# Gated rows summed on TensorE, both diagonal spectrum products on VectorE, and a planner that follows the buffers' turns

## The chip, the core and the metric

The kernel runs on one core of a Trainium2 chip. A core has TensorE (PE in the profile, with its weight loads as PEld), VectorE (DVE), ScalarE (ACT), GpSimd (POOL), and SyncE (SP), which issues most of the DMAs. The metric is the device time of one launch in microseconds. Before the change the median of three runs is 759.34 us (757.93 to 760.80).

## The reference

Four layers act on a sequence of 2048 positions and 512 channels. Layers A (gated) and B (a state-space filter made from exponentials) alternate; both end in a causal convolution over the whole sequence, done by a Fourier transform of length 4096.

```python
def _A_ref(q, k, v, shift_k, ssm_k, ssm_D):
    k_pad = jnp.pad(k, ((0, 0), (ks - 1, 0), (0, 0)))
    k_shift = jnp.zeros_like(k)
    for t in range(ks):                                   # ks = 4
        k_shift = k_shift + k_pad[:, t:t + S, :] * shift_k[:, ks - 1 - t][None, None, :]
    kv = k_shift * v
    ...                                                   # y = long convolution of kv with ssm_k
    y = y + kv * ssm_D[None, None, :]
    return q * y

def _B_ref(u, log_A_real, A_imag, C_real, C_imag, log_dt, D_skip):
    ...                                                   # C = (C_real + i C_imag) dt
    P = jnp.exp((A * dt[:, None])[:, :, None] * pos[None, None, :])
    K = 2.0 * jnp.einsum("dn,dnl->dl", C, P).real
    ...                                                   # y = long convolution of u with K
    return y + u * D_skip[None, None, :]

x = A_q
x = x + _A_ref(_layernorm(x, axis=-1), A_k, A_v, A_shift_k, A_ssm_k, A_ssm_D)
x = x + _B_ref(_layernorm(x, axis=-1), ...)
x = x + _A_ref(_layernorm(x, axis=-1), A_k, A_v, A_shift_k, A_ssm_k, A_ssm_D)
x = x + _B_ref(_layernorm(x, axis=-1), ...)
```

In layer A the sequence that is convolved, `kv`, depends on the inputs alone, not on x. So the long convolution of A is computed once and used by both A layers. The "gated rows" of this document are `kv`: four shifted copies of k, each times a tap, summed, and the sum times v.

## The kernel before

The program has three parts.

1. A short opening in program order: it loads the filter parameters and prepares rates and phases (line 177 in the profile, where operations are issued as they are recorded).
2. A planned part. Here every operation is only recorded (`Planner.record`), and `flush` issues them all in an order that `plan` works out (line 319 in the profile). Two generators feed it, interleaved by `run_steps`. The first, `stream`, builds the filter taps of layer B in 64 units, and then their spectra. The second, `diagonal`, makes the gated rows and the spectra of A's filter, and then runs A's long convolution.
3. The two B layers with the second A update between them, again in program order (line 177).

One unit of `taps` goes through these tiles: `pa` (angles, PSUM, two buffers) from a matmul, rounded by VectorE to `y`, `y` subtracted by a second matmul with `minus`, a negative unit matrix; ScalarE turns `pa` into sines and cosines (`ab`, `tt`); VectorE makes `e2` and GpSimd the two halves of `xy`; a contraction on TensorE sums them in `pk`. Eight units are a round; before each round six exponentials `m` are made from matmuls `pm`. A spectrum is made of `kk` (input), `pf` and `pu` (matmul results), `zk` (transposed) and `pc` (stored to `spec`).

The gated rows come in 16 groups of 32 channels. `gated` loads a tile `kvt` of 39 rows (19 of k, 16 of v, 4 of taps) and does eight elementwise operations of 128 by 512 elements on it: four products with the taps, three sums and the product with v. The mask `KVE` puts operations 1, 2, 4 and 7 on GpSimd and the others on VectorE, for 15 groups; the first group is all on GpSimd. Each operation reads what the one before it wrote in `u` or `tb`.

The long convolution (`convolution`, with `inplace` for A) takes pairs of frequency chunks: a matmul result `pu`, the diagonal products with the filter spectrum `kab`, a second matmul `pi`, a copy back, a transpose `w`, and the result `po`. The spectrum has two parts: ScalarE copies `pu` to the tile `sw` and GpSimd multiplies `sw` by one part, while VectorE multiplies `pu` by the other part into `vv`.

The planner takes a cost for each operation (`cost`) and goes through time: for each engine it takes the recorded operation that can start first, and the earliest of these is placed next. A tile can start when its tag has a free buffer; before the change it counts free buffers of a tag, in whatever order they come free. PSUM has one bank of tag `c1` (here for `po`), two double banks of tag `f1`, two of `pa` and one of `pk`.

Of the kernel before, what the change touches and what calls it, by code (L numbers as in the profile page):

```python
# [108 lines left out]
class Planner:  # L109
# [69 lines left out]

    def cost(self, op):  # L180
        name, a, k = op.calls[0]
        aps = [x for x in list(a) + list(k.values()) if hasattr(x, "tensor")]
        free = lambda x: int(np.prod([c for _, c in x.ap[1:]])) if len(x.ap) > 1 else 1
        n = max(free(x) for x in aps)
        if name == "dma_start":
            size = 4 * int(np.prod([c for _, c in aps[0].ap]))
            return (450 if op.engine == "D" else 600), 1500 + size / 290, size
        big = [x for x in aps[1:] if free(x) > 1]
        psum = [x.space == PSUM for x in big]
        if op.engine == "T":  # L190
            total, each = 0, 0
            for _, b, _ in op.calls:
                d = free(b[2]) * (1 if b[2].dtype == F32R else 4) / 2.4
                area = b[1].ap[0][1] * free(b[1]) / 16384
                total, each = total + d * area, max(each, d)
            return max(total, each), max(total, each) + 230, 0
        if op.engine == "V":
            alone = len(big) == 1 and not psum[0] and name in ("tensor_copy", "tensor_scalar", "tensor_scalar_mul")
            o = 60 + n * (0.52 if alone else 1.06)
            return o, o + 85, len(big) > 1 and not any(psum)  # L200
        if op.engine == "S":
            o = n / 1.2 + (50 if all(psum) else 184)
            if any(hasattr(k.get(x), "tensor") for x in ("scale", "bias")):
                o = n / 1.2 + (186 if name == "activation" and len(big) == 1 else 280)
            return o, o + 105, 0
        o = 100 + 2.2 * n if name.startswith("tensor_tensor") or name in ("tensor_mul", "tensor_add", "tensor_sub") else 100 + 0.9 * n
        return o, o + 50, n > 1

    def plan(self):
        ops = self.ops  # L210
        last_use, slots, queue = {}, {}, {}
        for op in ops:
            for t in op.uses:
                last_use[t.name] = op.n
        pending = [len(op.before) + len(op.ordered) for op in ops]
        follow = [[] for _ in ops]
        for op in ops:
            for o in list(op.before) + op.ordered:
                follow[o.n].append(op)
        users = {}  # L220
        for op in ops:
            for t in op.uses:
                users.setdefault(t.name, []).append(op.n)
                if len(users[t.name]) == 1 and t.tag_meta is not None:
                    queue.setdefault(t.tag, []).append(t)
        left = {n: len(u) for n, u in users.items()}
        taken = {tag: 0 for tag in queue}
        head = {tag: 0 for tag in queue}
        owner = {n: u[0] for n, u in users.items()}
        live = set()  # L230
        free = {e: 0.0 for e in self.engines}
        ready = [0.0] * len(ops)
        start, end = {}, {}
        avail = {e: [] for e in self.engines}
        lanes, server, lock = [0.0] * 8, 0.0, {"V": 0.0, "G": 0.0}
        costs = [self.cost(op) for op in ops]
        frees = {tag: [] for tag in queue}
# [3 lines left out]
        waiting = len(ops)  # L241
        while waiting:
            best = None
            for e, l in avail.items():
                pick = None
                for n in l:
                    op, t = ops[n], max(free[e], ready[n])
                    ok = True
                    for u in op.uses:
                        if u.name in live or u.tag_meta is None:  # L250
                            continue
                        tag = u.tag
                        q = queue[tag]
                        if q[head[tag]].name != u.name:
# [6 lines left out]
                        fr = frees[tag]  # L261
                        if len(fr) and u.tag_meta.bufs - taken[tag] <= len(fr):
                            t = max(t, sorted(fr)[0])
                    if not ok:
                        continue
                    if e == "D":
                        t = max(t, min(lanes))
                    if costs[n][2] and e in "VG":
                        t = max(t, lock["G" if e == "V" else "V"])
                    if pick is None or (t, n) < pick:  # L270
                        pick = (t, n)
                if pick is not None and (best is None or pick[0] < best[0]):
                    best = (pick[0], pick[1], e)
            assert best is not None, "plan is stuck"
            t, n, e = best
            op = ops[n]
            avail[e].remove(n)
            for u in op.uses:
                if u.name not in live and u.tag_meta is not None:
                    live.add(u.name)  # L280
                    taken[u.tag] += 1
                    head[u.tag] += 1
                    fr = frees[u.tag]
                    if len(fr) and u.tag_meta.bufs - taken[u.tag] < len(fr):
                        fr.remove(min(fr))
            o, lat, extra = costs[n]
            start[n] = t
            free[e] = t + o
            end[n] = t + lat
            if e == "D" or op.calls[0][0] == "dma_start":  # L290
                server = max(server, t + o) + extra / 290
                end[n] = max(t + o + 1500, server + 1200)
                if e == "D":
                    i = lanes.index(min(lanes))
                    lanes[i] = end[n]
            elif extra and e in "VG":
                lock[e] = t + o
            for u in op.uses:
                left[u.name] -= 1
                if not left[u.name] and u.tag_meta is not None:  # L300
                    taken[u.tag] -= 1
                    frees[u.tag].append(end[n])
            for f in follow[n]:
                pending[f.n] -= 1
                ready[f.n] = max(ready[f.n], end[n] + self.RELEASE[f.engine] if op in f.before else start[n] + o)
                if not pending[f.n]:
                    avail[f.engine].append(f.n)
            waiting -= 1
        self.length = max(end.values())
        return sorted(range(len(ops)), key=lambda n: (start[n], n))  # L310

    def flush(self):
        last = {}
        for n in self.plan():
# [16 lines left out]
def kernel(ctx: ExitStack, tc: tile.TileContext, out, x_in, kv_in, ssmk_in, ssmd_in,  # L331
# [174 lines left out]
    def convolution(which, pools, steps, finish, lag, ahead, nk, ns, nw, inplace, zlast=None, late_step=None, first_b=False):  # L506
# [12 lines left out]
        for s in range(-2 * NCH, NS + lag + NCH + 1):  # L519
# [312 lines left out]
    with ExitStack() as actx:  # L832
# [31 lines left out]
        KVE = 0b10010110  # L864
# [6 lines left out]
        def kv_steps():  # L871
            for grp in range(KV0, 16):
                yield from gated(grp, KVE)
# [54 lines left out]
        def diagonal():  # L928
            kvs = kv_steps()
            for q in range(NQ):  # L930
                for i, _ in enumerate(spectrum_quarter(0, q, ssmk_in, ap, zlast, ZA)):
                    if q == 0 and i == 1:
                        for grp in range(KV0):
                            for _ in gated(grp, 255):
# [271 lines left out]
```

## Time and profile before

| | |
|---|---|
| median of three runs | 759.34 us |
| the profiled execution | 758.29 us, of which its span 756.2 us |
| mean granted TensorE clock | 0.814 |
| opening, until the first exponentials | 0 to 48.7 us |
| rounds 1 to 4 of the taps, with the gated rows | 48.7 to 262 us |
| rounds 5 to 8, with A's long convolution from about 300 us on | 262 to 510 us |
| both B layers, second A update | 510 to 756 us |

The profile's page gives busy times and shares of the span. A row of the view by stretches has the stretch, its length, the busy time of PE, PEld, DVE, ACT and POOL with the count of instructions in brackets, the granted TensorE clock as a share of full speed, the DMA share and the bytes moved. A row of the groups has engine, operation, tiles, shapes and count, then the busy time of all, the mean ns of one, and the idle time of that engine just before them with what ended it. A row of the waits has who waited for whom, the us in total, how often, and the longest.

### The profile page before, as it was taken

Reading aid. Unit: us, or ns where it says so; the run is one execution under the profiler, and the core shown is the slowest. Engines: PE = TensorE matmul, PEld = TensorE weight load, DVE = VectorE, ACT = ScalarE, POOL = GpSimd, SP = SyncE. Lnnn points to the kernel's source line nnn. Section 1 sums busy time; section 2 is a strip of 40 time slices with the busy share of each in tenths; the row PEclk is TensorE's granted clock in tenths of the full one; section 3 lists DMA queues with packets and bytes.
Section 4 is the critical chain, followed back from the end, with each engine's and each line's share of the span. In section 5 each row is a group of like instructions: output and inputs, shape, how many; then the busy total and the mean of one; then the engine's idle time right before and its main releaser. Section 6 shows DMA issues by size and latency. Waiting matters only on the chain. (4 is left out here: it accounts for less than half of the span.)

```text
span 756.2 us, 20631 instructions
## 1 busy us (share of the span) xinstructions
PE 527.1 (70%) x8440; PEld 306.3 (40%) x8440; DVE 513.7 (68%) x930; ACT 421.1 (56%) x784; POOL 407.6 (54%) x378
## 2 busy tenths in 40 slices
PE   1356476467778688698877878563798880689984
PEld 0024243223426344464343455331465640256662
DVE  6765876748764458366777728764578889978864
ACT  4138447437547777975746388234673436837441
POOL 3756868688676576575448248500454530255551
PEclk9998565566665559889997879865999996889999
DMA  9888986346556315366577566669587713057764
GB/s 250 232 201 215 295 195 210 99 114 177 154 164 203 130 49 147 89 226 212 148 212 227 184 158 193 178 213 280 213 295 227 254 60 135 0 198 251 260 204 98
DMA packets 74497, 138.93 MB, mean 184 GB/s; under 512 B 8092, under 2 KB 37156, under 8 KB 72356
## 3 DMA queue, kind: packets, MB, share of 16 engines
q1 hardware_dynamic: 73540, 135.21, 60.0%
q0 software_dynamic: 864, 2.43, 1.1%
q8 instruction: 66, 1.08, 0.6%
q14 instruction: 27, 0.22, 0.1%
HBM read 97.75 MB, written 39.85 MB: 182 GB/s over the span
## 5 line engine op out<-in xcount | busy, mean ns | idle before, releaser
L319 POOL TENSOR_TENSOR xy<-tt,m 128x512 f32<-128x512 f32 x128 | 152.9, 1217 | 74.0 <-issue 30.1
L177 POOL TENSOR_TENSOR sw<-sw,kab 128x512 f32<-128x512 f32 x64 | 80.7, 1281 | 118.2 <-ACT sw L177 117.1
L319 ACT ACTIVATE m<-pm 128x1024 f32<-128x1024 f32 x48 | 46.7, 1029 | 66.3 <-PE pm L319 66.2
L319 PE MATMUL pf<-kk,w 64*128 64x512 f32 x128 | 57.3, 945 | 34.3 <-POOL kk L319 18.5
L319 PE MATMUL pk<-xy,e 128*32 128x64 f32 x2048 | 56.4, 271 | 20.2 <-POOL xy L319 18.5
L319 DVE TENSOR_TENSOR e<-pa,m 128x512 f32<-128x512 f32 x64 | 43.7, 682 | 38.8 <-ACT pa L319 15.9
L319 PE MATMUL pa<-tt,rw 64*128 64x512 f32 x64 | 41.4, 650 | 35.1 <-DVE e L319 34.1
L177 ACT COPY ie<-pi 128x1024 f32<-128x1024 f32 x32 | 32.5, 1014 | 57.4 <-PE pi L177 57.4
L319 PEld LDWEIGHTS pk<-xy,e 128*32 128x32 f32 x2048 | 43.3, 140 | 51.0 <-POOL xy L319 26.7
L177 DVE TENSOR_TENSOR vv<-pu,kab 128x512 f32<-128x512 f32 x64 | 40.9, 677 | 31.1 <-ACT sw L177 28.4
L319 ACT ACTIVATE ab<-pa 128x512 f32<-128x512 f32 x64 | 38.3, 598 | 39.0 <-PE pa L319 38.9
L319 DVE TENSOR_SCALAR y<-pa 128x512 fp32r<-128x512 f32 x64 | 43.5, 682 | 23.7 <-PE pa L319 22.5
L319 POOL TENSOR_TENSOR sw<-sw,kab 128x512 f32<-128x512 f32 x32 | 40.5, 1284 | 34.5 <-ACT sw L319 28.7
L319 DVE STREAM_TRANSPOSE zk<-pf 128x512 f32<-128x512 f32 x64 | 41.8, 690 | 24.0 <-PE pf L319 24.0
L319 POOL TENSOR_TENSOR u<-u,tb 128x512 f32<-128x512 f32 x32 | 44.3, 1388 | 24.3 <-DVE u L319 11.5
L177 PE MATMUL pf<-u,w 64*128 64x512 f32 (+1 forms) x136 | 39.6, 676 | 24.7 <-ACT u L177 17.0
L319 PE MATMUL pa<-y,minus 128*128 128x512 f32 x64 | 40.3, 629 | 23.1 <-DVE y L319 22.9
L177 PE MATMUL pi<-sw,mm 64*64 64x128 f32 x1024 | 52.3, 269 | 2.9 <-issue 2.9
L177 PE MATMUL pi<-vv,mm 64*64 64x128 f32 x1024 | 52.9, 274 | 0.5 <-DVE vv L177 0.4
L319 PE MATMUL pu<-zk,w 64*64 64x128 f32 x1024 | 48.6, 347 | 3.8 <-ACT m L319 1.5
L177 ACT COPY sw<-pu 128x1024 f32<-128x1024 f32 x32 | 32.3, 1014 | 29.8 <-PE pu L177 29.8
L319 PEld LDWEIGHTS pu<-zk,w 64*64 64x64 f32 x1024 | 40.3, 177 | 17.6 <-issue 10.1
(140 smaller groups left out, 1246.3 us busy)
## 6 DMA issues: line engine op xcount, KB each, us to landing
kab<-spec SPq DMA_DIRECT2D x94, 512.0 KB, 4.8
spec<-pc SPq DMA_DIRECT2D x64, 256.0 KB, 3.0
kvt<-kv_in SPq DMA_DIRECT2D x32, 312.0 KB, 5.2
kk<-ssmk_in SPq DMA_DIRECT2D x32, 128.0 KB, 3.6
xr<-x_in SPq DMA_DIRECT2D x8, 512.0 KB, 5.9
kv_d<-u SPq DMA_DIRECT2D x16, 256.0 KB, 4.2
kdram<-ks SPq DMA_DIRECT2D x64, 64.0 KB, 4.1
kk<-kdram SPq DMA_DIRECT2D x32, 128.0 KB, 3.0
```

The source lines that it names most:

```text
L177: op.ins = getattr(self.engines[key], name)(*a, **k).ins
L319: ins = getattr(self.engines[op.engine], name)(*a, **k).ins
```

## The change

It has three parts.

- `gated`: GpSimd makes the four products with the taps, each into its own half of two tiles (`prod`). TensorE adds them: four matmuls with `minus`, read as plain f32, accumulate the negative sum in a PSUM bank `kv` of tag `c1`. VectorE multiplies that by -1 and by v in one operation, and the result is stored. The mask is gone; all 16 groups go this way.
- `convolution`, for A alone: VectorE makes both diagonal products from `pu` in PSUM. The copy to `sw` by ScalarE and the product by GpSimd are gone there. The B layers are as before.
- `Planner`: a tile now waits for that earlier tile of its tag whose buffer it gets in turn (`prior`). The cost of a matmul depends on an assumed TensorE clock of 0.5 or 1 that follows the matmul work in windows of 3413 ns, and that of a DMA on the length of its runs. So the order of the whole planned part is another.

The third part of the program has the same instructions in the same order as before.

```diff
+    @staticmethod
+    def run(ap):
...
-            return (450 if op.engine == "D" else 600), 1500 + size / 290, size
+            run = min(self.run(x) for x in aps)
+            return (450 if op.engine == "D" else 600), 1500 + size / 290, size / (290 if run >= 512 else 200)
...
-            return max(total, each), max(total, each) + 230, 0
+            return max(total, each), 230, total
...
-    def plan(self):
+    def prepare(self):
...
+                    q = self.queue.setdefault(t.tag, [])
+                    self.prior.append(q[-t.tag_meta.bufs] if len(q) >= t.tag_meta.bufs else None)
+                    q.append(len(self.prior) - 1)
...
+    def plan(self, rank=None):
...
+                    for u in using[n]:
+                        if live[u] or prior[u] is None:
                             continue
...
-                        room = u.tag_meta.bufs - taken[tag]
-                        if room <= 0:
-                            ok = False
-                            break
...
+                        if left[prior[u]]:
                             ok = False
                             break
+                        t = max(t, idle[prior[u]] + self.RELEASE[e])
...
+            if e == "T":
+                k = int(t / 3413)
+                while window < k:
+                    clock = 1.0 if act.get(window, 0.0) >= 0.42 * 3413 else 0.5
+                    window += 1
+                o = o / clock
...
@@ convolution
-                    swapped[0] = S.copy(vvs[s // 2][1], pus[0])
+                    if not inplace:
+                        swapped[0] = S.copy(vvs[s // 2][1], pus[0])
                 wa, wb = vvs[s // 2]
-                G.tensor_mul(wb[:, c % 2], wb[:, c % 2], kabs[s][:, 1])
+                if inplace:
+                    V.tensor_mul(wb[:, c % 2], pus[0][:, c % 2], kabs[s][:, 1])
+                else:
+                    G.tensor_mul(wb[:, c % 2], wb[:, c % 2], kabs[s][:, 1])
                 V.tensor_mul(wa[:, c % 2], pus[0][:, c % 2], kabs[s][:, 0])
...
-        def gated(grp, onpool):
+        def gated(grp):
             kvt = ap.tile([128, 39, 32], F32, name="kvt", tag="kab", bufs=NKA)
             by_half(kvt.rearrange("p t c -> p (t c)"), kv_in[grp])
-            u = ap.tile([128, 16, 32], F32, name="u", tag="vv", bufs=NSA // 2)
-            tb = ap.tile([128, 16, 32], F32, name="tb", tag="sw", bufs=NSA // 2)
-            e = [G if (onpool >> i) & 1 else V for i in range(8)]
-            sk = lambda j: kvt[:, 35 + j, :][:, None, :].to_broadcast([128, 16, 32])
-            kt = lambda j: kvt[:, j:j + 16, :]
-            e[0].tensor_mul(u, kt(3), sk(0))
-            e[1].tensor_mul(tb, kt(0), sk(3))
-            e[2].tensor_add(u, u, tb)
+            prods = [ap.tile([128, 2, 16, 32], F32, name="prod", tag=tag, bufs=NSA // 2) for tag in ("vv", "sw")]
+            kv = bank("kv")
+            for j in range(4):
+                G.tensor_mul(prods[j // 2][:, j % 2], kvt[:, 3 - j:19 - j, :],
+                             kvt[:, 35 + j, :][:, None, :].to_broadcast([128, 16, 32]))
+                T.matmul(kv, minus.bitcast(F32), prods[j // 2][:, j % 2].rearrange("p t c -> p (t c)"),
+                         start=j == 0, stop=j == 3)
+                if j % 2:
+                    yield
+            u = prods[0][:, 0].rearrange("p t c -> p (t c)")
+            V.scalar_tensor_tensor(u, kv, -1.0, kvt[:, 19:35, :].rearrange("p t c -> p (t c)"), op0=ALU.mult, op1=ALU.mult)
+            Q.dma_start(kv_d[grp], u)
             yield
-            e[3].tensor_mul(tb, kt(1), sk(2))
-            e[4].tensor_add(u, u, tb)
-            yield
-            e[5].tensor_mul(kt(2), kt(2), sk(1))
-            e[6].tensor_add(u, u, kt(2))
-            e[7].tensor_mul(u, u, kt(19))
-            Q.dma_start(kv_d[grp], u.rearrange("p t c -> p (t c)"))
-            yield
```

More of the change, by code (lines that the diff above doesn't have):

```diff
@@ L178, in record @@
         return op
+    @staticmethod
+    def run(ap):
+        dims = [tuple(d) for d in ap.ap] if ap.space == DRAM else [tuple(d) for d in ap.ap[1:]]
+        n = 1
+        for s, c in reversed(dims):
+            if c > 1 and s != n:
+                break
+            n *= c
+        return n
     def cost(self, op):
@@ L207, in cost @@
         return o, o + 50, n > 1
-    def plan(self):
+    def prepare(self):
         ops = self.ops
-        last_use, slots, queue = {}, {}, {}
+        self.costs = [self.cost(op) for op in ops]
+        self.follow = [[] for _ in ops]
         for op in ops:
-            for t in op.uses:
[L214 to L231, printed above, removed]
+            for o in op.before:
+                self.follow[o.n].append((op.n, True))
+            for o in op.ordered:
+                self.follow[o.n].append((op.n, False))
+        self.pending = [len(op.before) + len(op.ordered) for op in ops]
+        names, self.prior, self.queue = {}, [], {}
+        self.using, self.users = [], []
+        for op in ops:
+            l = []
+            for t in op.uses:
+                if t.tag_meta is None:
+                    continue
+                if t.name not in names:
+                    names[t.name] = len(self.prior)
+                    q = self.queue.setdefault(t.tag, [])
+                    self.prior.append(q[-t.tag_meta.bufs] if len(q) >= t.tag_meta.bufs else None)
+                    q.append(len(self.prior) - 1)
+                    self.users.append(0)
+                l.append(names[t.name])
+                self.users[names[t.name]] += 1
+            self.using.append(l)
@@ L235, in plan @@
         lanes, server, lock = [0.0] * 8, 0.0, {"V": 0.0, "G": 0.0}
-        costs = [self.cost(op) for op in ops]
-        frees = {tag: [] for tag in queue}
+        act, window, clock = {}, 0, 0.5
         for op in ops:
@@ L240, in plan @@
                 avail[op.engine].append(op.n)
-        waiting = len(ops)
-        while waiting:
+        for waiting in range(len(ops)):
             best = None
@@ L277, in plan @@
             avail[e].remove(n)
[L278 to L285, printed above, removed]
+            for u in using[n]:
+                live[u] = True
             o, lat, extra = costs[n]
@@ L297, in plan @@
                 lock[e] = t + o
[L298 to L307, printed above, removed]
@@ L308, in plan, with best @@
-            waiting -= 1
-        self.length = max(end.values())
+            for u in using[n]:
+                left[u] -= 1
+                idle[u] = max(idle[u], end[n])
+            for f, real in self.follow[n]:
+                pending[f] -= 1
+                ready[f] = max(ready[f], end[n] + self.RELEASE[ops[f].engine] if real else start[n] + o)
+                if not pending[f]:
+                    avail[ops[f].engine].append(f)
+        self.length = max(end)
         return sorted(range(len(ops)), key=lambda n: (start[n], n))
+    def best(self):
+        return self.plan()
@@ L312, in flush @@
     def flush(self):
         last = {}
-        for n in self.plan():
+        self.prepare()
+        for n in self.best():
             op = self.ops[n]
@@ L872, in kv_steps @@
             for grp in range(KV0, 16):
-                yield from gated(grp, KVE)
+                yield from gated(grp)
         def steps_a(q):
```

59 lines of the change are left out of this document (33 added, 26 removed).

## The prediction

> **What bounds the kernel now.** I read the page's shares first, then the busy time in four stretches: opening, taps with gated rows (48.7 to 262), taps with the first long convolution (262 to 510), the rest.
>
> ```profile
> span 756.2 us, 20631 instructions
> PE 527.1 (70%) x8440; PEld 306.3 (40%) x8440; DVE 513.7 (68%) x930; ACT 421.1 (56%) x784; POOL 407.6 (54%) x378
> ```
> ```profile
> core 0: us, PE busy (x) PEld busy (x) DVE busy (x) ACT busy (x) POOL busy (x), PEclk, DMA share, GB/s
> 0.00:48.70 48.70, 11.31 (x20) 3.40 (x21) 30.90 (x45) 11.36 (x17) 25.50 (x37) 1.00 0.87 230
> 48.70:262.00 213.30, 145.49 (x1748) 80.47 (x1745) 140.03 (x207) 127.57 (x264) 155.18 (x133) 0.65 0.64 179
> 262.00:510.00 248.00, 192.81 (x3323) 113.61 (x3323) 160.65 (x292) 159.59 (x299) 136.60 (x130) 0.84 0.58 172
> 510.00:756.20 246.20, 177.47 (x3352) 108.78 (x3352) 182.12 (x389) 122.54 (x205) 90.33 (x79) 0.90 0.59 191
> ```
>
> No engine is full. POOL leads the second stretch (155.2 of 213.3, 73%), PE the third (78%). The change leaves the last stretch as it is, so about 246 us can't move. What stands between POOL and full in the second stretch, by the waits there:
>
> ```profile
> ACT m L319 <- PE pm L319: 64.2, 9, 26.0
> POOL u L319 <- DVE u L319: 33.4, 13, 5.8
> POOL u L319 <- DVE tb L319: 8.9, 4, 3.3
> ```
>
> POOL waits 42.3 us (33.4 + 8.9) for VectorE inside the gated rows. ACT's 64.2 us are its pauses between rounds of eight units, when the exponentials wait for the last products.
>
> **Part 1, the gated rows.** Their groups of the second stretch alone:
>
> ```profile
> L319 POOL TENSOR_TENSOR u<-u,tb 128x512 f32<-128x512 f32 x28 | 38.8, 1388 | 20.6 <-DVE tb L319 8.9 <-DVE u L319 8.4 <-POOL xy L319 1.4
> L319 POOL TENSOR_TENSOR u<-u,kvt 128x512 f32<-128x512 f32 x14 | 20.5, 1462 | 25.0 <-DVE u L319 25.0
> L319 DVE TENSOR_TENSOR kvt<-kvt 128x512 f32<-128x512 f32 x14 | 19.6, 1401 | 0.2
> L319 POOL TENSOR_TENSOR tb<-kvt 128x512 f32<-128x512 f32 x13 | 17.4, 1335 | 0.0
> L319 DVE TENSOR_TENSOR tb<-kvt 128x512 f32<-128x512 f32 x14 | 14.9, 1064 | 3.5 <-POOL u L319 3.5
> L319 DVE TENSOR_TENSOR u<-kvt 128x512 f32<-128x512 f32 x14 | 14.0, 997 | 2.3 <-DMA kv_d<-u 2.0 <-POOL u L319 0.3
> L319 DVE TENSOR_TENSOR u<-u,kvt 128x512 f32<-128x512 f32 x14 | 11.1, 796 | 0.2
> ```
> The same operations when undisturbed, minimum first:
> ```profile
> L319 POOL TENSOR_TENSOR tb<-kvt x17: 1251/1259/1722, 22.0 to 226.7; 128x512 f32<-128x512 f32 x17
> L319 DVE TENSOR_TENSOR tb<-kvt x15: 648/685/3160, 27.7 to 245.4; 128x512 f32<-128x512 f32 x15
> L319 DVE TENSOR_TENSOR vv<-pu,kab 128x512 f32<-128x512 f32 x32 | 21.8, 683 | 31.4 <-PE pu L319 21.3 <-ACT sw L319 9.8
> ```
> *POOL*: removed 38.8 + 20.5 + 17.4 = 76.7; added 14 groups of 4 products at 1.25 = 70. So 155.2 - 6.7 = 148.5, and its waits for VectorE go: 58.1 idle - 42.3 = 15.8. POOL alone would need 164 us. *VectorE*: removed 59.6, added 14 x 0.68 (one factor from PSUM, as in the vv row) = 9.5, so 140 falls to 90.
>
> *PE*: 56 new exact f32 matmuls of 128x128 by 512. The trace has none among other work; nearest are the idle matmuls and, clock low and high, pf (two halves side by side, 512 columns):
>
> ```profile
> 641.09 9.16 PE L177 MATMUL idle<-x,w 128*128 128x512 f32 x16 [17.61 <-issue]
> ```
> ```profile
> 184.61 2.08 PE L319 MATMUL pf<-kk,w 64*128 64x512 f32 x4
> 183.59 1.08 PE L319 MATMUL pk<-xy,e 128*32 128x64 f32 x32
> ```
> ```profile
> 361.70 1.09 PE L319 MATMUL pf<-kk,w 64*128 64x512 f32 x4
> ```
> ```profile
> 405.03 0.65 PE L319 MATMUL pk<-xy,e 128*32 128x64 f32 x32
> ```
>
> The 16 idle records are eight matmuls, 1.15 us each. So 1.1 us at full clock and 2.08 at half: 62 or 116 us for the 56. I take 1.1, nearest to the same shape; the ends stay in the range. The old work has the same two prices (pk 0.65 or 1.08, pf 1.09 or 2.08), warm about 0.57 of cold. If the clock is either full or half, a mean of 0.65 is 30% of the time at full and 70% at half, so the old 145.5 us would be 145.5 x (0.3 + 0.7 x 0.57) = 102 at full clock. Turned round for other means (the old divided by the share at full plus 0.57 of the share at half, the new with 1.1 / 2.08 = 0.53), PE needs 102 + 62 = 164 at full clock, 179 at 0.9, 210 at 0.75, 237 at 0.65. PE thus takes over from POOL, and its clock decides. The rounds show what a denser PE is granted:
>
> ```profile
> 104.70:163.70 59.00, 35.88 (x428) 19.75 (x428) 37.86 (x56) 31.12 (x65) 44.58 (x37) 0.60 0.55 151
> 163.70:220.90 57.20, 42.41 (x508) 21.14 (x508) 41.69 (x54) 32.96 (x69) 43.99 (x39) 0.70 0.58 167
> 300.60:356.40 55.80, 45.21 (x920) 30.51 (x920) 32.49 (x51) 40.29 (x73) 33.66 (x29) 0.88 0.54 166
> 356.40:434.70 78.30, 61.88 (x997) 32.77 (x995) 58.21 (x110) 43.98 (x80) 38.03 (x35) 0.87 0.66 199
> ```
> At 61% and 74% busy the clock is 0.60 and 0.70; at 81% and 79% it is 0.88 and 0.87. The new work makes PE denser than any of these, so I take 0.9 (179 us) and, since an in-order PE still waits for products, 90% busy: 199 us, 14 less than 213. The ends are 164 (-49) and 250 (237 at 95%, +37).
>
> Against this stand single windows of 3.4 us:
> ```profile
> 97.78:101.19 3.41, 3.41 (x39) 2.03 (x40) 1.84 (x4) 0.00 (x0) 3.41 (x4) 0.50 0.77 155
> 104.61:108.02 3.41, 1.82 (x40) 1.01 (x38) 3.38 (x11) 2.53 (x3) 2.72 (x3) 1.00 0.73 200
> 183.11:186.52 3.41, 3.41 (x37) 1.39 (x37) 3.41 (x3) 2.40 (x7) 3.41 (x4) 0.50 0.88 218
> ```
> ```profile
> 98.87 4.79 PE L319 MATMUL pf<-kk,w 64*128 64x512 f32 x12
> ```
> After this run of pf the clock is 1.00; yet at 183 PE is busy throughout and has 0.50. Which matmuls fill the time matters, and full-width ones, as the new are, precede the rise.
>
> [...]
>
> How PE's queue changes, at the first units (kv is the sum in PSUM, pa angles, pk the contraction, pu a spectrum). Before:
> ```order
> L319 MATMUL pu_276<-zk_229,w2_108 64x128 x16
> L319 MATMUL pa_281<-tt_208,rw_249 128x512
> L319 MATMUL pa_281<-y_282,minus_142 128x512
> L319 MATMUL pk_272<-xy_270,e2_271 32x64 x16
> L319 MATMUL pa_286<-tt_208,rw_249 128x512
> ```
> and now:
> ```order
> L342 MATMUL pu_279<-zk_229,w2_108 64x128 x16
> L342 MATMUL kv_284<-prod_282,minus_142 128x512
> L342 MATMUL pa_285<-tt_208,rw_252 128x512
> L342 MATMUL pa_285<-y_286,minus_142 128x512
> L342 MATMUL pk_275<-xy_273,e2_274 32x64 x16
> L342 MATMUL pa_290<-tt_208,rw_252 128x512
> L342 MATMUL kv_284<-prod_282,minus_142 128x512
> ```
> A kv matmul that waits for POOL's product now holds the next unit's angles behind it; a late POOL costs PE directly. The sum has one PSUM bank, so groups follow one another: 5.0 of products, a last matmul of 1.1 and VectorE's 0.7, 6.8 us for each of 14, 95 in all, well inside the stretch. SP issues as many loads and stores as before. In the opening, eight POOL products stand ahead of the fourth kk add, where there were eleven gated operations; I count 2 us saved, 0 to 4 possible.
>
> **Part 2, the diagonal products of the third stretch.**
> ```profile
> L319 POOL TENSOR_TENSOR sw<-sw,kab 128x512 f32<-128x512 f32 x32 | 40.5, 1284 | 34.5 <-ACT sw L319 28.7 <-PE pk L319 4.3 <-DMA kab<-spec 1.5
> L319 ACT COPY sw<-pu 128x1024 f32<-128x1024 f32 x16 | 16.2, 1014 | 17.4 <-DVE vv L319 14.6 <-PE pu L319 2.8
> ```
> POOL loses 40.5, ACT 16.2; VectorE gains 32 x 0.683 = 21.9 and reaches 182.5. For each of 16 pairs the way from pu to pi was a copy and two POOL products, 1.0 + 2.6 = 3.6; now four VectorE products, 2.7: at most 16 x 0.9 = 14 less. The handovers beside it (28.7, 14.6, 9.8) partly go. VectorE's queue at the first pair, before:
> ```order
> L319 TENSOR_TENSOR vv_749<-pu_748,kab_712 128x512
> L319 TENSOR_TENSOR e2_744<-pa_732,m2_721 128x512
> L319 TENSOR_TENSOR vv_749<-pu_748,kab_715 128x512
> L319 TENSOR_SCALAR y_757<-pa_756 128x512
> L319 TENSOR_TENSOR e2_760<-pa_740,m2_721 128x512
> ```
> and now:
> ```order
> L342 TENSOR_TENSOR sw_766<-pu_764,kab_728 128x512
> L342 TENSOR_TENSOR vv_765<-pu_764,kab_728 128x512
> L342 TENSOR_TENSOR sw_766<-pu_764,kab_731 128x512
> L342 TENSOR_TENSOR e2_760<-pa_748,m2_737 128x512
> L342 TENSOR_TENSOR vv_765<-pu_764,kab_731 128x512
> L342 TENSOR_SCALAR y_773<-pa_772 128x512
> ```
> Angles (y) and e2 of the taps wait behind two more products. I take -12 for the stretch, near the shorter way. The new plan itself changes no durations and can order better or worse; I price it at nothing within these terms and let it widen both ends; the ends are -30 (PE's 192.8 at 88%) and +22 (all new VectorE work on the path).
>
> **Sum.** The profiled execution took 758.3 us, 1.0 below the median of 759.3. 758.3 - 2 - 14 - 12 = 730.3; on the median's scale 731; I say 730.
>
> **Rivals.** *PE stays cold*: kv matmuls come singly between waits and do not lift the clock (the window at 183). At 0.65 the second stretch is 250, +37: 758.3 - 2 + 37 - 12 + 1 = 782. It decides below a clock of 0.83, where PE at 90% needs the old 213. For it: 0.60 to 0.70 now; against it: 0.87 at 80% busy. Chance 0.17. *VectorE becomes the bound in the third stretch* (74% even at the old length) and PE's clock is 0.85: 189 / 0.9 = 210, so -3, the opening -2, part 2 about -3: 751, chance 0.15. *Both come out well*: PE at 0.95 and 95% busy, 171 / 0.95 = 180, -33, and part 2 -25: 699, chance 0.16. *The parts cancel*, within 0.5% of 759.3 (what a measurement of this kernel can tell from no change): 0.07.
>
> **Numbers.** My forecast has 0.45, with a range of its own of 706 to 745. Faster: 0.45 + 0.16 + 0.15 = 0.76; same 0.07; slower 0.17. From 692 to 765 the range leaves out most of the cold case and the best of the good one.
>
> **What would show it.** Right: between the first exponentials and the last gated row, clock near 0.9, PE busy near 90%, POOL without waits for VectorE, that stretch some 14 us shorter; then no sw copies on ACT. Wrong: clock under 0.8 there with PE waiting for POOL's products, or VectorE over 85% busy in the third stretch.

## The result and the profile after

The changed kernel takes 750.13 us (median of four runs, 749.08 to 750.75), the kernel before, measured beside it, 758.63 (756.68 to 760.80): a ratio of 0.9886, 95% interval 0.9854 to 0.9917. It is faster by 8.5 us where 29 were forecast: clear of the noise, but only 1.1%. In this and all later ratios, runs more than 1.5% longer than the fastest run of the same kernel are left out.

The profiled execution after, its shares and its stretches (columns as before: stretch, length, busy PE, PEld, DVE, ACT, POOL, clock, DMA share, GB/s):

```profile
span 747.2 us, 20838 instructions
PE 553.5 (74%) x8568; PEld 307.6 (41%) x8568; DVE 508.5 (68%) x918; ACT 404.9 (54%) x768; POOL 350.1 (47%) x342
```
```profile
0.00:48.70 48.70, 18.05 (x29) 5.79 (x30) 32.10 (x38) 11.35 (x17) 19.19 (x32) 0.93 0.73 193
48.70:262.00 213.30, 173.13 (x1972) 82.78 (x1970) 120.72 (x173) 131.40 (x270) 150.87 (x143) 0.88 0.68 190
262.00:510.00 248.00, 184.89 (x3218) 109.85 (x3218) 178.55 (x349) 141.26 (x282) 89.79 (x88) 0.84 0.61 182
510.00:747.20 237.20, 177.44 (x3352) 109.19 (x3352) 177.17 (x359) 120.92 (x202) 90.28 (x79) 0.91 0.57 185
```

In the second stretch PE's clock rose from 0.65 to 0.88 and POOL's work fell as forecast. But VectorE, which was to fall to 90 us, is busy for 120.7. Its four longest operations, the first from the opening and three from the planned part, from the timeline (start, duration, engine, line, operation):

```profile
22.19 10.35 DVE L177 TENSOR_TENSOR hl<-ph,hl 128x512 fp32r<-128x512 f32 x1 [0.69 <-ACT hl L177]
85.36 9.56 DVE L342 CAST rw<-raw 128x256 fp32r<-128x256 f32 x1
174.37 7.02 DVE L342 CAST rw<-raw 128x256 fp32r<-128x256 f32 x1
198.25 6.70 DVE L342 CAST rw<-raw 128x256 fp32r<-128x256 f32 x1
```
The same subtraction took 1.59 us before; it began beside one product of POOL, which then paused:

```profile
22.23 1.59 DVE L177 TENSOR_TENSOR hl<-ph,hl 128x512 fp32r<-128x512 f32 x1 [0.68 <-ACT hl L177]
22.01 1.26 POOL L319 TENSOR_TENSOR tb<-kvt 128x512 f32<-128x512 f32 x1
26.36 1.26 POOL L319 TENSOR_TENSOR u<-u,tb 128x512 f32<-128x512 f32 x1 [3.09 <-DVE u L319]
```
All 16 casts, from the view by tile (ns minimum, median, maximum), before and then after:
```profile
L319 DVE CAST rw<-raw x16: 274/404/1242, 47.5 to 405.1; 128x256 fp32r<-128x256 f32 x16
```
```profile
L342 DVE CAST rw<-raw x16: 269/372/9560, 52.9 to 406.1; 128x256 fp32r<-128x256 f32 x16
```

Here is POOL's timeline around the first two, and PE's after the second:
```profile
21.97 2.48 POOL L342 TENSOR_TENSOR prod<-kvt 128x512 f32<-128x512 f32 x2
24.42 0.24 POOL L342 TENSOR_TENSOR kk<-kk,dr 1x32 f32<-1x32 f32 x1
24.63 7.36 POOL L342 TENSOR_TENSOR prod<-kvt 128x512 f32<-128x512 f32 x6
31.96 0.69 POOL L342 TENSOR_TENSOR kk<-kk,dr 1x32 f32<-1x32 f32 x1
43.57 0.24 POOL L342 TENSOR_TENSOR kk<-kk,dr 1x32 f32<-1x32 f32 x1 [10.92 <-DMA kk<-ssmk_in]
...
85.13 2.48 POOL L342 TENSOR_TENSOR prod<-kvt 128x512 f32<-128x512 f32 x2
87.58 4.55 POOL L342 TENSOR_TENSOR xy<-tt,m 128x512 f32<-128x512 f32 x4
92.09 0.24 POOL L342 TENSOR_TENSOR kk<-kk,dr 1x32 f32<-1x32 f32 x1
92.30 2.47 POOL L342 TENSOR_TENSOR prod<-kvt 128x512 f32<-128x512 f32 x2
94.74 0.29 POOL L342 TENSOR_TENSOR kk<-kk,dr 1x32 f32<-1x32 f32 x1
```
```profile
95.67 0.76 PE L342 MATMUL pa<-tt,rw 64*128 64x512 f32 x1 [7.55 <-DVE e L342]
```

POOL works without a gap from 21.97 to 32.65, and the subtraction ends at 32.54. It works from 85.13 to 95.03, and the cast ends at 94.92. The other two end at 181.39 and 204.95, where POOL's runs end at 181.24 and 205.06. A cast of 0.27 us thus holds VectorE's queue for up to 9.56, with `e`, the transposes and `y` behind it; PE then waits 7.55 us for `e`. The subtraction delays the store of the rows, and the first exponentials start at 53.85 us instead of 48.74. The four operations took 33.6 us in place of some 2.5 (1.59 for the subtraction, 0.27 to 0.4 for a cast), 31 too many.

Not every cast beside such a run is held. Seven casts began in a run of POOL that went on for 5 us or more; three were held to its end, and these four were let in after the instruction that POOL was at, 5.0 to 7.3 us before the run's end:
```profile
54.04 0.91 DVE L342 CAST rw<-raw 128x256 fp32r<-128x256 f32 x1 [0.22 <-DMA raw<-rows_d]
70.16 0.96 DVE L342 CAST rw<-raw 128x256 fp32r<-128x256 f32 x1
126.66 1.03 DVE L342 CAST rw<-raw 128x256 fp32r<-128x256 f32 x1
143.10 0.42 DVE L342 CAST rw<-raw 128x256 fp32r<-128x256 f32 x1
```

### The profile page after: what moved, and what is told of

Its sections match the earlier page's. It is cut to its first block, busy times and chain, and to the rows that moved or that the text cites. A ratio compares the mean times of both kernels' runs of the same rounds, so it can differ in the third digit from the quotient of the medians.

```text
span 747.2 us, 20838 instructions
## 1 busy us (share of the span) xinstructions
PE 553.5 (74%) x8568; PEld 307.6 (41%) x8568; DVE 508.5 (68%) x918; ACT 404.9 (54%) x768; POOL 350.1 (47%) x342
## 5 line engine op out<-in xcount | busy, mean ns | idle before, releaser
L342 POOL TENSOR_TENSOR xy<-tt,m 128x512 f32<-128x512 f32 x128 | 148.5, 1185 | 143.9 <-ACT tt L342 64.0
L177 POOL TENSOR_TENSOR sw<-sw,kab 128x512 f32<-128x512 f32 x64 | 80.6, 1280 | 119.3 <-ACT sw L177 112.1
L342 PE MATMUL kv<-prod,minus 128*128 128x512 f32 x128 | 80.3, 720 | 9.3 <-DVE prod L342 7.1
L342 POOL TENSOR_TENSOR prod<-kvt 128x512 f32<-128x512 f32 x64 | 79.8, 1269 | 15.6 <-DMA kv_d<-prod 9.7
L342 PE MATMUL pf<-kk,w 64*128 64x512 f32 x128 | 45.0, 755 | 39.9 <-DMA kk<-ssmk_in 21.0
L342 PE MATMUL pa<-tt,rw 64*128 64x512 f32 x64 | 35.2, 554 | 23.1 <-DVE e L342 23.0
L342 PE MATMUL pk<-xy,e 128*32 128x64 f32 x2048 | 47.3, 240 | 2.9 <-POOL xy L342 1.5
L177 PE MATMUL pu<-zu,w 64*64 64x128 f32 x1024 | 37.2, 281 | 14.3 <-DVE zu L177 12.2
L342 PEld LDWEIGHTS pk<-xy,e 128*32 128x32 f32 x2048 | 36.0, 121 | 28.6 <-issue 19.8
L342 PE MATMUL pu<-zk,w 64*64 64x128 f32 x1024 | 40.0, 301 | 9.3 <-DVE zk L342 6.6
```

The lines of the kernel that those rows point to most:

```text
L177: op.ins = getattr(self.engines[key], name)(*a, **k).ins
L342: ins = getattr(self.engines[op.engine], name)(*a, **k).ins
```

## The experiments

All ratios are to the kernel before, run beside each experiment on the same chip (its median there was 753 to 754 us, 5 us less than beside the change), with 95% intervals; the difference of two of them is uncertain by some 0.5 to 0.9 points. Some diffs are shortened.

**First theory**: VectorE's operations that work in SBUF alone are held up while GpSimd works without a pause; the rest of the forecast was right. **Rival**: PE's in-order queue waits at the ends of the rounds, and the casts lie beside that.

**Casts on ScalarE.** When the finished plan is issued, each `tensor_copy` of VectorE becomes ScalarE's `copy`:

```diff
             op = self.ops[n]
+            if op.engine == "V" and op.calls[0][0] == "tensor_copy":
+                op.engine, op.calls = "S", [("copy",) + op.calls[0][1:]]
```


> The changed kernel with the 16 casts rw<-raw on ScalarE instead of VectorE, at the places in the program where they stood; PE's, GpSimd's and SyncE's orders are those of the changed kernel. Theory (VectorE operations that use SBUF alone are held up while GpSimd works without a pause; three casts of the changed kernel took 9.56, 7.02 and 6.70 us instead of 0.27, together 22 us too many): no cast takes over 1 us, PE no longer waits 7.6 us for e near 95 us, the second stretch is 6 to 15 us shorter, 735 to 744 us in all. If other VectorE operations with two SBUF inputs take over the waiting, one of them now shows 5 us or more and the gain stays under 3 us. Rival (PE's stretch is long because its in-order queue waits at the ends of the rounds, and the casts lie beside that): 747 to 753, with ACT's waits for PE's pm near 54 us as before.

Measured: ratio 0.9519 (0.9450 to 0.9589), from three of its six runs (709.92 to 717.62 us), 3.7 points below the change. The exponentials of round 8 start at 395.3 us instead of 426.3. The rival falls: 16 casts on another engine are worth some 28 us. That is also more than the 6 to 15 that the theory expected: the casts themselves were 22 us too long, and beside that PE's work in rounds 1 to 4 shrank from 166.1 to 155.5 us as its clock rose from 0.88 to 0.94. The subtraction into `hl` is still held, at the same 10.35 us.

**The parts of the change, each left out.** The plan alone (gated rows and diagonal products as before):

> The kernel before with nothing but the new planner (rotating buffers, new costs): gated rows and both diagonal products as they were. The prediction priced the plan at nothing: 755 to 763 against 759. Rival (the plan alone brings the whole gain, and the two edits nothing): 748 to 752. Rival (the plan costs, the edits bring more than the whole shows): over 765.

Measured: 0.9923 (0.9884 to 0.9962), between the two expectations: the plan alone is worth 6 us. The change without the new gated rows:

> The changed kernel with the gated rows of before (eight operations shared by GpSimd and VectorE, no sum in PSUM); new plan and new diagonal products stay. Theory (the new gated rows free GpSimd and warm PE, but give about half of it back in the held-up VectorE operations): 753 to 760, with the clock of the second stretch at 0.65 to 0.72 and no cast over 2 us. Rival (the gated rows bring nothing, all of the gain is the third stretch's and the plan's): 747 to 752. By the prediction's own term (14 and 2 us): 766.

Measured: 0.9980 (0.9938 to 1.0022), the longest cast 1.32 us as expected, the second stretch's clock 0.77, above the 0.65 to 0.72 expected. The change without the new diagonal products:

> The changed kernel with the diagonal products of before (copy on ScalarE, two products on GpSimd and two on VectorE); new plan and new gated rows stay. By the prediction's term (12 us): 762. Theory from the milestones of the two traces (the third stretch ends 9 us earlier in the changed kernel and begins 5 us earlier): 752 to 757. Rival (the new products only move the wait to VectorE and bring nothing): 748 to 752, with the third stretch as long as in the changed kernel.

Measured: 1.0027 (0.9985 to 1.0069), with the same hold-ups as in the change: casts of 8.78, 7.04 and 6.71 us, and 2.81 and 8.06 for the two subtractions into `hl`. On the scale of 759 us that is 761, near what the prediction's term of 12 gives, and not the 752 to 757 of the theory.

**The same with the casts on ScalarE.** If moving the casts helped by itself, it would help where GpSimd makes no long runs too. The kernel before:

> The kernel before with nothing but its 16 casts rw<-raw on ScalarE; the orders of PE, GpSimd and SyncE stay. Theory (the casts cost much only where GpSimd works without a pause, which it does not in the kernel before, where the longest took 1.24 us): 0.985 to 1.005 of the kernel before. Rival (a cast on VectorE's queue costs the rounds their 5% whatever GpSimd does): 0.95 to 0.96.

Measured: 0.9945 (0.9912 to 0.9978). The change without the new gated rows:

> New plan and new diagonal products, the gated rows of before, and the casts rw<-raw on ScalarE. Without the casts moved this kernel took 0.998 of the kernel before. Theory (no long run of GpSimd, so nothing to win): 0.98 to 1.00; the new gated rows are then worth 3 to 4%, the difference to 0.952. Rival (moving the casts brings 4 to 5% by itself): 0.95 to 0.96.

Measured: 0.9875 (0.9803 to 0.9947), but from two of its twelve runs (738.65 and 747.43 us). The median of all twelve is 754.21, that of the kernel before 754.13. The change without the new diagonal products:

> New plan and new gated rows, the diagonal products of before, and the casts rw<-raw on ScalarE. Without the casts moved this kernel took 1.003 of the kernel before, its casts 30.0 us. Theory: 0.955 to 0.975, since the held-up casts go and the diagonal products are worth the prediction's 12 us (1.6%) at most. Rival (the diagonal products bring nothing once the casts are out of the way): 0.950 to 0.955.

Measured: 0.9642 (0.9588 to 0.9695). So moving the casts brings 0.6 and at most 1.1 points with the old gated rows, 3.7 and 3.9 with the new ones. The table puts the parts together:

| | casts on VectorE | casts on ScalarE |
|---|---|---|
| kernel before | 1 | 0.9945 |
| new plan | 0.9923 | not run |
| new plan, diagonal products | 0.9980 | 0.9875 |
| new plan, gated rows | 1.0027 | 0.9642 |
| the whole change | 0.9886 | 0.9519 |

What a part is worth depends on what stands beside it. With the casts on VectorE, either part added to the new plan alone loses 0.6 to 1.0 points. Added to the other part, the new gated rows bring 0.9 points (7 us) and the diagonal products 1.4 (11 us). With the casts on ScalarE the gated rows bring 3.6 points (27 us, more if all twelve runs count), the diagonal products 1.2 (9 us). Part of this is the order and not the edit: with old gated rows and new diagonal products, the plan leaves a whole spectrum (128 matmuls of `pu`) behind the last copy of `ya`, and the third part's first matmul, at 512.04 us in the changed kernel, waits for its copies:

```profile
517.59 2.93 PE L177 MATMUL pf<-u,w 64*128 64x512 f32 x6 [4.72 <-ACT pc L342]
```

**The subtractions as well.** The two operations into `hl` go to GpSimd, ahead of its first products; every other order stays:

```diff
-    split(1, ph, V)
-    split(3, t2, V)
+    split(1, ph, G)          # issued so; planned as VectorE's
+    split(3, t2, G)
```


> The changed kernel with the casts on ScalarE and the two subtractions into hl, of which one took 10.35 us on VectorE, on GpSimd ahead of its first products; every other engine's order stays. Theory (the held-up subtraction delays the store of the rows and with it the first exponentials, at 54 us instead of 48.7): first exponentials at 46 to 50 us, 0.940 to 0.948 of the kernel before. Rival (the opening waits for the loads of kk, which take as long either way): first exponentials at 53 to 55, 0.950 to 0.955.

Measured: 711.09 us, 0.9453 (0.9409 to 0.9496), first exponentials at 47.12 us. With no operation held up, the kernel is 5.5% faster than before.

**What kind of cast is held up.** The cast stays on VectorE but takes the two blocks of a row in turn:

```diff
-        V.tensor_copy(rows[gi], raw)
+        V.tensor_copy(rows[gi].rearrange("p a b -> p b a"), raw.rearrange("p a b -> p b a"))
```


> The changed kernel with the casts still on VectorE, but with the two blocks of 128 elements of a row read and written in turn (neighbouring elements 128 apart) instead of straight through; every order stays. Theory A (a one-input cast is held up behind GpSimd only because, straight through, it runs in a fast form, 0.27 us for 256 elements): each cast takes 0.3 to 1.5 us, none more, and the time is 0.950 to 0.960 of the kernel before, as with the casts on ScalarE. Theory B (every VectorE operation that reads and writes SBUF alone is held up): the longest casts stay at 6 to 10 us, 0.983 to 0.993.

Measured: 0.9894 (0.9843 to 0.9945). The casts by tile:
```profile
L342 DVE CAST rw<-raw x16: 402/656/9694, 54.2 to 409.4; 128x256 fp32r<-128x256 f32 x16
```
The undisturbed cast is now 0.40 us instead of 0.27, and it is held up as long as before, for up to 9.69 us: theory A falls, as far as the longer time marks another form of the cast, which the run does not show.

**A planner that knows.** Its plan now keeps one-input operations apart in time from GpSimd's products, as it did two-input ones (subtractions on GpSimd as above):

```diff
-            return o, o + 85, len(big) > 1 and not any(psum)
+            return o, o + 85, n >= 128 and (alone or len(big) > 1 and not any(psum))
```


> The changed kernel with a planner that is told that casts and other one-input operations on VectorE can't run beside GpSimd's products (it knew this of two-input operations alone), so that it places them elsewhere; casts stay on VectorE, the two hl subtractions are on GpSimd. If the planner's model is right: no cast over 1.5 us, 0.940 to 0.955 of the kernel before. If VectorE is held up whatever the planner believes, because GpSimd's next product goes first each time: casts of 5 us or more remain, 0.965 to 0.990.

Measured: 0.9708 (0.9664 to 0.9752); casts of 7.25 and 3.59 us remain, as the second expectation has it.

**The casts planned on ScalarE**, subtractions on GpSimd as above:

```diff
-        V.tensor_copy(rows[gi], raw)
+        S.copy(rows[gi], raw)
```


> The casts given to ScalarE before the program is planned, so that the planner makes room for them, and the two hl subtractions on GpSimd: a version meant to be fast. Theory: as with the casts moved afterwards, 0.937 to 0.950 of the kernel before (0.945 there). Rival (another plan is as good as a draw): 0.95 to 0.965.

Measured: 717.03 us, 0.9500 (0.9454 to 0.9546), on the border of the two expectations. It is not better than moving the casts after planning.

**Longer runs of GpSimd.** Each gated product is issued twice:

```diff
-            for i, (name, a, k) in enumerate(op.calls):
+            twice = op.engine == "G" and op.calls[0][0] == "tensor_mul" and "prod" in op.calls[0][1][0].tensor.name
+            for i, (name, a, k) in enumerate(op.calls * (1 + twice)):
```


> The changed kernel with each of GpSimd's 64 gated products computed twice in a row, so that GpSimd's runs without a pause are longer; VectorE's, PE's and SyncE's orders stay. Theory (VectorE's operation waits until GpSimd's run ends): the subtraction into hl that took 10.35 us beside 8 products takes about 20 us beside 16, and the casts near 85 and 198 us take more than 9.6 and 6.7 us; GpSimd's work alone grows by 80 us, the whole by 30 to 90 us. Rival (the hold-up has a length of its own): it stays near 10 us.

Measured: 765.64 us (two runs), 1.0145 (1.0082 to 1.0207), some 20 us more than the change, and both expectations fall. VectorE's and POOL's timeline, and the casts by tile:
```profile
23.72 1.58 DVE L177 TENSOR_TENSOR hl<-ph,hl 128x512 fp32r<-128x512 f32 x1 [0.68 <-ACT hl L177]
25.23 1.75 DVE L177 TENSOR_TENSOR hl<-t,hl 128x512 fp32r<-128x512 f32 x1
```
```profile
23.50 5.95 POOL L342 TENSOR_TENSOR prod<-kvt 128x512 f32<-128x512 f32 x4
29.41 0.24 POOL L342 TENSOR_TENSOR kk<-kk,dr 1x32 f32<-1x32 f32 x1
29.62 15.41 POOL L342 TENSOR_TENSOR prod<-kvt 128x512 f32<-128x512 f32 x12
```
```profile
L342 DVE CAST rw<-raw x16: 262/371/934, 53.5 to 423.6; 128x256 fp32r<-128x256 f32 x16
```
GpSimd works from 23.50 to 45 us without a visible pause, and yet the subtraction takes 1.58 us and no cast over 0.93. What differs stands in GpSimd's program (in brackets what an instruction waits for; Pool is GpSimd's own semaphore). The changed kernel:

```
L342 TENSOR_TENSOR prod_240<-kvt_239 128x512 [waits DMAHW1_49,DMAHW0_49]
L342 TENSOR_TENSOR prod_240<-kvt_239 128x512
L342 TENSOR_TENSOR prod_241<-kvt_239 128x512 x2
L342 TENSOR_TENSOR prod_235<-kvt_233 128x512 x2
```
and with the products doubled:
```
L342 TENSOR_TENSOR prod_240<-kvt_239 128x512 [waits DMAHW1_49,DMAHW0_49]
L342 TENSOR_TENSOR prod_240<-kvt_239 128x512 [waits Pool_49]
L342 TENSOR_TENSOR prod_240<-kvt_239 128x512
L342 TENSOR_TENSOR prod_240<-kvt_239 128x512 [waits Pool_49]
```
A second product writes what the first wrote, so it waits for the first to end. In the trace such waits take time: four products with two of them take 5.20 us (from 87.70), where twice two without one, at 2.48 in the changed kernel, are 4.96. **New theory**: VectorE is held up only while GpSimd's instructions follow one another without such a wait; each wait for the last one's end lets VectorE in.

By the run at 85.13 above it has to be the last one's end. Two of its four `xy` wait for GpSimd's own semaphore too, but for an earlier instruction that had ended: the four follow without a gap (4.55 us, where a single one takes 1.18), and the cast stays held, for 9.56 us.

**That wait alone.** Every GpSimd instruction of the planned part (247) waits for the one before it; nothing else changes:

```diff
-                        self.edge(ins, last[op.engine])                          # order only
+                        self.edge(ins, last[op.engine], op.engine == "G")        # GpSimd: wait for its end
```


> The changed kernel with one wait more: every GpSimd instruction waits until the one before it on GpSimd has ended. Orders, engines and work are those of the changed kernel; casts and hl subtractions stay on VectorE. New theory (VectorE is held up only while GpSimd's instructions follow one another without a wait for the last to end; the kernel with the doubled products had such waits, since the second product writes what the first wrote, and nothing was held up in it): no VectorE operation over 2 us after 25 us, first exponentials at 47 to 54 us, the rounds as in the kernel with the casts on ScalarE, 0.945 to 0.965 of the kernel before, the waits themselves costing GpSimd some 20 to 60 ns for each of its 342 instructions. Rival (it was the doubled products' longer time that spread the work, not their waits): three casts of 6 us or more and the 10 us subtraction stay, 0.985 to 1.00.

Measured: 712.39 us, 0.9460 (0.9415 to 0.9506). The casts by tile, one of them beside POOL's products, and the stretches between the same events as before (first exponentials, those of round 5, near the end of the planned part):
```profile
L342 DVE CAST rw<-raw x16: 271/428/1234, 44.7 to 368.4; 128x256 fp32r<-128x256 f32 x16
```
```profile
72.85 2.63 POOL L342 TENSOR_TENSOR prod<-kvt 128x512 f32<-128x512 f32 x2
75.56 0.24 POOL L342 TENSOR_TENSOR kk<-kk,dr 1x32 f32<-1x32 f32 x1
```
```profile
74.87 0.76 DVE L342 CAST rw<-raw 128x256 fp32r<-128x256 f32 x1
```
```profile
0.00:47.10 47.10, 20.62 (x38) 6.51 (x38) 24.33 (x41) 11.82 (x18) 22.81 (x35) 0.93 0.85 235
47.10:222.00 174.90, 155.55 (x1921) 74.08 (x1920) 97.44 (x168) 126.51 (x265) 151.81 (x140) 0.95 0.77 222
222.00:480.00 258.00, 190.75 (x3280) 112.61 (x3274) 185.31 (x361) 152.98 (x306) 93.07 (x90) 0.84 0.62 184
```
The same four engines with the same work in the same order, and these waits, are 4.3 points (32 us) faster, about as much as the four operations had lost. This is the cure in one line. No cast takes over 1.23 us now, nor any VectorE operation over 1.3 us after the first 25 us. A pair of products takes 2.63 us instead of 2.48 with one wait inside, and the next instruction follows 0.08 us later, so a wait costs GpSimd some 0.1 to 0.15 us.

For the subtraction this run is no test: it took 0.69 us, but had ended at 25.18 us, before GpSimd's first product at 25.36. That it is not held beside products with such waits, the doubled products show (1.58 us).

The same wait where nothing is held up:

> The kernel with casts on ScalarE and the hl subtractions on GpSimd (0.9453 of the kernel before, no VectorE operation held up) with the same wait ahead of every GpSimd instruction. It shows what the waits themselves cost where there is nothing for them to free: 0.945 to 0.960 if they cost GpSimd 20 to 60 ns each; under 0.94 would mean that something else than the four operations was held up too.

Measured: 0.9492 (0.9443 to 0.9542) against 0.9453 without the waits; POOL's busy time is 359.3 against 351.7 us. The waits cost little, and there is no sign that anything else was held up.

How long a VectorE operation takes beside GpSimd's work differs in the changed kernel's trace: the four casts that were let in took 0.42 to 1.03 us and had waited for one instruction, the three others and the subtraction took 6.70 to 10.35 us, where one product takes 1.27.

## Why the prediction was wrong

Measured between events (first exponentials; those of round 5; the last copy of `ya`, some 5 us ahead of the end of the planned part), the profiled executions give the table below. The kernel before took 5 us less beside the run with the waits than beside the change, so that column's gains are a few us too large.

| us | before | after | with the waits | predicted change |
|---|---|---|---|---|
| opening | 48.7 | 53.9 (+5.1) | 46.6 (-2.1) | -2 |
| rounds 1 to 4 | 213.3 | 202.8 (-10.5) | 174.9 (-38.4) | -14 |
| rounds 5 to 8, convolution | 243.2 | 239.6 (-3.6) | 237.2 (-6.0) | -12 |
| rest | 251.0 | 250.9 | 253.7 | 0 |

- **The clock, the matmul and POOL** were right: 0.88 against 0.9. Not all of the rise is the new matmuls': with the new plan alone, rounds 1 to 4 have 0.72. A kv sum's pair of records takes 1.12 to 1.13 us at clock 1.00 (near 85 us), 1.1 was taken; the group of 64 matmuls has the mean 80.3 / 64 = 1.25, some of them at clock 0.50, with 2.05 to 2.08 us (at 97.47 and 100.46). POOL has 150.9 us where 148.5 were worked out, and its waits for VectorE inside the gated rows are gone.
```profile
L342 PE MATMUL kv<-prod,minus 128*128 128x512 f32 x128 | 80.3, 720 | 9.3 <-DVE prod L342 7.1 <-POOL prod L342 2.1
```
- **The step that failed** is "its waits for VectorE go", counted as pure gain for POOL. The new independent products follow one another without a wait for the last one's end, and VectorE stood behind them for 31 us. From this step came the opening (-2 became +5.1; with the waits it is -2.1), and PE "90% busy" and VectorE "falls to 90" in rounds 1 to 4: PE was busy for 166 of 202.9 us, 82%; with the waits for 155.6 of 174.9, 89%, and VectorE for 97.4. That GpSimd's old waits, for VectorE and for its own last result, had kept VectorE's hold-ups short (3.16 us at most in the kernel before) was not tried by itself, and they are not the whole account: there too casts were let in beside runs without a pause (one of 1.03 us at 63.46, beside four `xy` that follow one another for 4.66 us).
- **The diagonal products' term** was the second to fail: -12 was put on the third stretch, and rounds 5 to 8 lost 3.6 us, 6.0 with the waits. The edit took only 2 to 3 us there (239.6 against 242.5 in the profile with the old products). Another 3 lie behind the last `ya`: with the old products 64 matmuls of a spectrum come after it, and the third part's first matmul comes at 517.91 us instead of 512.04. These 6 us are all that the two profiles differ by; the ratios give 11, uncertain by 4, so the 12 was right by the times at best, and only beside the new gated rows.
- **The plan, priced at nothing**, was worth 6 us (0.9923; the interval reaches from 3 to 9). In its trace rounds 1 to 4 take 201.3 us. This too hid how much was lost: with the hold-ups, the new gated rows added nothing to that (202.8).
- **PE's work** was put too high: 179 us at clock 0.9, 171 at 0.95, and 155.6 measured at 0.95. Of these the kv sums have 63.4, near the 62 of the prediction, so it is the old work that was put too high. So without the hold-ups the stretch, 174.9 us, beats the forecast's 199.
- **The window at 183**, from which the prediction took that it matters which matmuls fill the time, was read wrongly. The granted clock of that trace changes at 181.00 and at 191.24; in stretches cut there, PE is busy for 67% and 75% at clock 0.50, then throughout, and clock 1.00 follows. The third stretch has the same matmuls as the window at 183 (nearly all of them the 32 of `pk` and the 4 records of `pf`), so these rows show no difference by the kind of matmul:
```profile
181.00:184.41 3.41, 2.30 (x34) 1.39 (x34) 2.47 (x3) 2.83 (x8) 3.41 (x5) 0.50 1.02 289
184.41:187.82 3.41, 2.55 (x17) 0.80 (x9) 3.41 (x5) 1.64 (x5) 3.41 (x3) 0.50 0.47 114
187.82:191.24 3.42, 3.42 (x37) 1.36 (x37) 2.16 (x4) 0.00 (x0) 2.57 (x3) 0.50 0.00 0
191.24:194.65 3.41, 3.41 (x88) 2.69 (x90) 2.66 (x5) 2.12 (x5) 0.00 (x0) 1.00 0.24 83
```
- **The rivals.** PE did not stay at 0.65: its clock was 0.88. "VectorE becomes the bound in the third stretch", 751 us, has the time but not the cause: VectorE is busy for 72% of it, and the same 72% in the kernel that takes 712. Once nothing is held up the edits are worth 41 us (0.9460 of 758.6 is 718), which lies between the forecast's 730 and the 699 of "Both come out well".

Left open: what lets a cast in. Four of seven were let in beside runs without a pause and three were not, and what tells them apart is not known. So the theory says when a hold-up can come, not when it does. Shown is that none was held once every planned GpSimd instruction waited for the one before it.

## What to carry to other kernels

When a change frees an engine from its waits, ask who used the gaps; look in the new trace for operations whose maximum is many times their minimum, since a mean over a group hides them. Where GpSimd and VectorE both work in SBUF, as here, where a cast of 0.27 us took up to 9.56, try to keep short, urgent VectorE operations off the stretches in which GpSimd has independent work, or to make each GpSimd instruction wait for the one before it: here that was worth 32 us. Leave each part of a change out in turn, and do it again when a loss has been found: the gated rows showed 7 us of worth with the hold-ups and 27 without.

## What was not expected of the hardware

- A VectorE operation of 0.27 or 0.7 us was held up for 6.7 to 10.35 us, until GpSimd's run of instructions ended; small GpSimd operations in between (1 by 32 elements, 0.24 us) did not let it in. Four other casts beside such runs waited for one instruction only (0.42 to 1.03 us).
- With every planned GpSimd instruction waiting for the end of the one before it, no cast took over 1.23 us; a wait for an earlier one that had ended left no gap, and in the run at 85.13 us let nothing in. With waits for the last one's end inside 8 pairs of products (each product issued twice) GpSimd worked from 23.50 to 45 us without a visible pause, and VectorE's subtraction beside it took 1.58 us.
- Both a subtraction with two inputs (10.35 us) and a cast with one (9.56 us) were held up, and the cast also in its slower form (0.40 us undisturbed, 9.69 held).
